# Filter rows of the "plus" side in one transfer of long rows, and the filter product as one VectorE op for each part of the filter

## The chip, the cores and the metric

The kernel runs on one core of a Trainium2 chip. The metric is device time in microseconds (us); each kernel was run several times, and all runs quoted are in the fast state (granted TensorE clock 0.986 to 1.0 in the profiled runs). Before the change the median was 134.44 us over 3 runs.

The profile shows the work of five engines, each with its own instruction stream in the program. In this kernel PE does the matmuls (786 in the profile before) and writes the memory PSUM. VectorE (DVE in the profile, 127 instructions) and ScalarE (ACT, 146) read PSUM and write the memory SBUF; such a copy out of PSUM is called an eviction. GpSimd (POOL, 33) works on tiles in SBUF here. SyncE (SP) issues nearly all transfers (DMA). The program fixes the order of each stream and lets streams wait for each other through semaphores. The kernel uses PSUM as 8 banks.

## The reference, cut to what matters

```python
# x: (1, 2048, 512) bf16;  w_r, w_i: (2048, 257) bf16
X = rfft2(layernorm(x));  X = X * (w_r + 1j * w_i)        # <- the filter
h = x + irfft2(X)
y = h + token_mlp(layernorm(h))                            # w1: 2048x1376, w2: 1376x2048
```

The kernel makes the two transforms as matmuls with constant matrices. The filter has a real part `w_r` and an imaginary part `w_i`. In the filter step the groups of 257 frequencies are handled in eight stages u = 0..7, four groups to a stage. In each stage:

1. `f2`: matmuls from Y, evicted by ScalarE as CS (two evictions per stage, `cs_2u` and `cs_2u+1`);
2. `x`: eight matmuls from CS into two PSUM banks. I write x(u) for those of stage u;
3. `v`: VectorE multiplies the PSUM result with both parts of the filter and writes V to SBUF. I write V(u);
4. `g1`: sixteen matmuls from V, evicted by ScalarE as PQ.

After stage 7 come g2, g3, a second layernorm, and the two large matmuls of the MLP.

## The kernel before

The author's builder records operations with their costs and priorities. A list scheduler then fixes each engine's order and the PSUM banks, once, from modelled durations. So a change in one operation can move others.

```python
# PSUM classes: how many units of each may be open at once
K = Builder(nc, {"f1": 6, "f2": 2, "x": 2, "g1": 2, ...})

add("W", [NP, NG, 2, LW], bf, rw)          # filter in SBUF: partition, group, part, 257
V_SPLIT = (0, 7)                            # stages whose product is made in two halves

# filter loads, in three chunks of stages; per part w and component comp (cut: minus rows, row 32)
for w, dram in ((0, A_w_r), (1, A_w_i)):
    for comp in range(2):
        d = W[comp::4, g0:g0 + ng, w, :]    # 32 partitions, rows of 257 bf16 = 514 B
        lst.append(dma(f"ld_wp{ch}_{w}{comp}", d, bass.AP(dram.tensor, g0 * LW, [[64 * LW, 32], [LW, ng], [1, LW]]), ...))
...
# the product: one VectorE op for both parts (two halves in stages 0 and 7)
wt = W[:, g0 + h * ng:g0 + h * ng + ng, :, :]
win = bass.AP(wt.tensor, wt.offset + 1, [list(wt.ap[0]), [LW, 2 * ng], [1, 2], [2, NP]])
vout = V[:, g0 + h * ng:g0 + h * ng + ng, :, :].rearrange("p g w l -> p (g w l)")
def tt(eng, bank, ...):
    s = bass.AP(s.tensor, s.offset, [list(s.ap[0]), [256, ng], [0, 2], [1, 256]])   # PSUM, each group read twice
    return eng.tensor_tensor(vout, s, win, ALU.mult)
K.op(f"v_{u}_{h}", "dve", tt, ins=[wt], outs=[vout], occ=50.0 + 2130.0 / nh, lat=170.0 + 2130.0 / nh, ...)
```

## Time and profile before

| | before |
|---|---|
| time, median of 3 (range) | 134.44 us (134.16 to 134.53) |
| profiled span, mean clock | 133.0 us, 1.000 |
| VectorE from 22 to 40 us | busy 17.88 of 18.00 us |
| V ops | 10 (six of 2048 elements, four of 1024) |
| packets of all transfers | 16,648 |

The first view is the page's packet line and its group line for V. Columns of a group line: line, engine, operation, output<-inputs, shapes, count; then busy us and mean ns of one; then idle time before them and what ended most of it.

```profile
DMA packets 16648, 22.16 MB, mean 167 GB/s; under 512 B 2720, under 2 KB 12960, under 8 KB 16128
...
L735 DVE TENSOR_TENSOR V<-ps,W 128x2048 bf16<-128x2048 f32 (+1 forms) x10 | 17.9, 1856 | 0.9 <-PE ps L527 0.9
```

The timeline of VectorE (start, us, engine, line, operation, count, and in brackets idle before it and what ended that) shows the stretch without a break:

```profile
20.39 0.69 DVE L708 CAST CS<-ps 128x512 bf16<-128x512 f32 x1 [0.92 <-PE ps L527]
22.02 17.88 DVE L735 TENSOR_TENSOR V<-ps,W 128x1024 bf16<-128x1024 f32 x10 [0.93 <-PE ps L527]
43.17 0.42 DVE L786 TENSOR_TENSOR TT<-ps,X 128x256 f32<-128x256 f32 x1 [3.27 <-PE ps L527]
```

Ten products follow one another from 22.02 to 39.90 us. Then VectorE has nothing for 3.27 us while g1, PQ, g2, EO and g3 run. V's only wait is the 0.93 us before the first, and it is for PE, not for a transfer.

The chain of waits that ended last (start, us, what):

```profile
19.15 2.77 PE ps L527 x25
...
22.02 1.04 DVE V L735
...
23.16 15.62 DVE V L735 x8
...
68.59 61.14 PE ps L527 x282
```

V lies on the chain op by op. From 43.17 to 68.5 VectorE is on it again (second layernorm), and the end is 61 us of PE without a gap.

PE's timeline around x(6), the seventh block of eight "CS,EM" matmuls:

```profile
34.66 0.61 PE L527 MATMUL ps<-CS,EM 64*128 64x256 bf16 x8
35.21 0.39 PE L527 MATMUL ps<-EM,Y 128*128 128x256 bf16 x2
35.44 0.72 PE L527 MATMUL ps<-EM,V 128*128 128x128 bf16 x10
```

x(6) is done at 35.27 us, while VectorE still works on V(5) (V(6) starts at 35.34, so x(6) is ready only just in time); the g1 matmuls that wait for V(5) stand behind it, at 35.44. So V(6) can follow V(5) at once.

SyncE's issues of the last filter loads and of the MLP's weights (both tensors appear as W):

```profile
22.61 3.28 SPq L517 DMA_DIRECT2D W<-in_A_w_i_dram  x4
...
30.52 16.34 SPq L517 DMA_DIRECT2D W<-in_B_w_dram  x15
```

### The profile page before, as it was taken

To read this page: it belongs to the slowest core of one execution; us is meant where nothing else is said; L and a number is where in the kernel's file an instruction comes from. 1 tells how busy PE (TensorE), PEld (TensorE's weight loads), DVE (VectorE), ACT (ScalarE), POOL (GpSimd) and SP (SyncE) were. 2 spreads that over 40 slices of the span, in tenths; PEclk is the share of its full clock that TensorE was granted. 3 is DMA by queue.
4 is the path that set the end of the run, shared out by engine and by line. 5 is a ranking of instruction groups with operands and counts; after the bars stand their busy time and mean duration, and the time that the engine had idled before them with its cause. 6 is when DMAs were issued, how large, how long until landed. Compare 5 with 4: busy or idle time off the path is not lost.

```text
span 133.0 us, 2023 instructions
## 1 busy us (share of the span) xinstructions
PE 125.4 (94%) x786; PEld 75.3 (57%) x786; DVE 69.2 (52%) x127; ACT 63.4 (48%) x146; POOL 12.2 (9%) x33
## 2 busy tenths in 40 slices
PE   6999989999987979999999999999999999999990
PEld 2356756878656726644434444456666666666660
DVE  0379975999990999999970000000242332423322
ACT  4569976878966999986679322222000000000000
POOL 0288830000300000000000000000000000000000
PEclk9999999999999999999999999999999999999999
DMA  3999698999999999992000000000111112111121
GB/s 94 335 370 382 178 276 229 304 317 264 411 430 430 398 411 409 419 281 89 0 0 0 0 0 0 5 0 0 39 39 64 55 39 81 42 59 59 39 79 39
DMA packets 16648, 22.16 MB, mean 167 GB/s; under 512 B 2720, under 2 KB 12960, under 8 KB 16128
## 3 DMA queue, kind: packets, MB, share of 16 engines
q1 hardware_dynamic: 16352, 21.52, 47.3%
q10 hardware_dynamic: 288, 0.52, 1.3%
q8 instruction: 6, 0.10, 0.3%
q14 instruction: 2, 0.02, 0.0%
HBM read 19.95 MB, written 2.10 MB: 166 GB/s over the span
## 4 chain that ended last, share of the span: by engine, by line
PE 51%; DVE 33%; ACT 8%; DMA 5%; issue 1%; SPq 1%; DVEq 0%; ACTq 0%
PE ps L527 50%; DVE V L735 13%; DVE H L795 7%; DMA X<-in_A_x_dram 5%; ACT Y L545 5%; DVE TT L786 4%; DVE TT L788 4%; DVE HH L800 4%; ACT rs L545 1%; ACT FS L545 1%; DVE st L649 1%; SPq L517 1%; DVE OUT L825 1%; ACT PQ L545 0%; PE ps L617 0%
## 5 line engine op out<-in xcount | busy, mean ns | idle before, releaser
L527 PE MATMUL ps<-HH,W 128*128 128x512 bf16 (+1 forms) x176 | 40.7, 379 | 1.2 <-DVE HH L800 0.9
L527 PE MATMUL ps<-GT,W 128*128 128x512 bf16 (+1 forms) x176 | 38.2, 379 | 0.0
L825 DVE SCALAR_TENSOR_TENSOR OUT<-ps,B2f,H 128x512 bf16<-128x512 f32 x16 | 12.0, 750 | 48.7 <-PE ps L527 48.7
L527 PEld LDWEIGHTS ps<-GT,W 128*128 128x128 bf16 (+1 forms) x176 | 25.4, 144 | 12.7
L527 PEld LDWEIGHTS ps<-HH,W 128*128 128x128 bf16 (+1 forms) x176 | 17.2, 100 | 21.2 <-DVE HH L800 1.9
L735 DVE TENSOR_TENSOR V<-ps,W 128x2048 bf16<-128x2048 f32 (+1 forms) x10 | 17.9, 1856 | 0.9 <-PE ps L527 0.9
L545 ACT ACTIVATE GT<-ps,B1f 128x512 bf16<-128x512 f32 (+1 forms) x11 | 7.1, 688 | 14.6 <-PE ps L527 14.6
L545 ACT ACTIVATE JK<-H,nm 128x512 bf16<-128x512 bf16 x16 | 11.6, 724 | 3.0 <-DVE H L795 2.9
L617 PE MATMUL ps<-ZT 128*128 128x512 bf16 x34 | 11.3, 479 | 1.3 <-DVE ZT L613 1.2
L649 DVE BATCH_NORM_STATS2 st<-X 128x6 f32<-128x512 bf16 x14 | 9.3, 668 | 5.3 <-DMA X<-in_A_x_dram 5.3
L795 DVE TENSOR_TENSOR H<-ps,TT 128x512 bf16<-128x512 f32 x16 | 10.9, 681 | 0.0
L545 ACT ACTIVATE PQ<-ps 128x512 bf16<-128x512 f32 x16 | 8.9, 603 | 3.5 <-PE ps L527 3.2
L545 ACT ACTIVATE EO<-ps 128x512 bf16<-128x512 f32 x16 | 9.3, 599 | 0.9 <-PE ps L527 0.9
L527 PE MATMUL ps<-EM,V 128*128 128x128 bf16 x128 | 9.2, 219 | 0.5 <-DVE V L735 0.5
L527 PE MATMUL ps<-EM,PQ 128*128 128x256 bf16 x64 | 9.0, 273 | 0.7 <-ACT PQ L545 0.7
L545 ACT ACTIVATE CS<-ps 128x512 bf16<-128x512 f32 x15 | 8.3, 608 | 2.1 <-PE ps L527 2.1
L527 PE MATMUL ps<-EM,Y 128*128 128x256 bf16 x64 | 8.7, 273 | 0.4 <-ACT Y L545 0.4
L527 PEld LDWEIGHTS ps<-EM,V 128*128 128x128 bf16 x128 | 7.5, 98 | 2.3 <-issue 1.4
L629 POOL TENSOR_SCALAR FS<-FP,rs 128x256 bf16<-128x256 bf16 x9 | 8.3, 935 | 1.3 <-ACT rs L545 1.3
L527 PE MATMUL ps<-FS,X 128*128 128x256 bf16 x64 | 8.3, 273 | 0.1
L786 DVE TENSOR_TENSOR TT<-ps,X 128x256 f32<-128x256 f32 x16 | 6.7, 416 | 3.3 <-PE ps L527 3.3
L527 PEld LDWEIGHTS ps<-EM,PQ 128*128 128x128 bf16 x64 | 6.2, 98 | 2.9 <-ACT PQ L545 0.9
(36 smaller groups left out, 80.3 us busy)
## 6 DMA issues: line engine op xcount, KB each, us to landing
W<-in_B_w_dram SPq DMA_DIRECT2D x4, 1376.0 KB, 11.0
W<-in_B_w_dram SPq DMA_DIRECT2D x10, 512.0 KB, 17.6
out_dram<-OUT SPq DMA_DIRECT2D x16, 128.0 KB, 1.7
W<-in_A_w_r_dram SPq DMA_DIRECT2D x4, 257.0 KB, 4.3
W<-in_A_w_i_dram SPq DMA_DIRECT2D x4, 257.0 KB, 5.0
X<-in_A_x_dram SPq DMA_DIRECT2D x4, 256.0 KB, 5.8
X<-in_A_x_dram SPq DMA_DIRECT2D x2, 512.0 KB, 7.7
W<-in_A_w_r_dram SPq DMA_DIRECT2D x4, 192.8 KB, 3.5
```

The lines of the kernel that those rows point to most:

```text
L517: return eng.dma_start(dst, src)
L527: return K.op(name, "pe", lambda eng, bank: eng.matmul(outf(bank), lhsT, rhs, start=start, stop=stop), ins=ins or [lhsT, rhs], occ=occ, la ...
L545: return eng.activation(dst, s, func, **kw)
L617: return K.op(name, "pe", lambda eng, bank: eng.matmul(ps[:, bank, :], ZT[:, 0:NP], ZT[:, :], start=True, stop=True), ins=[ZT[:, :]], occ= ...
L629: dve(f"fs{i}", lambda eng, bank: eng.tensor_scalar(FS[:, i, :, :], FP[:, i, :, :], rs, None, op0=ALU.mult), [FP[:, i, :, :], rs], [FS[:, ...
L649: dve(f"st_{i}", lambda eng, bank, i=i, x=x: eng.bn_stats(ST[:, i, 0:6], x), [x], [ST[:, i, 0:6]], 512, prio=25)
L735: return eng.tensor_tensor(vout, s, win, ALU.mult)
L786: dve(f"tl_{s2}", lambda eng, bank, tt=tt, xl=xl: eng.tensor_tensor(tt[:, 0, :], ps[:, bank, 256:512], xl, ALU.add), [xl], [tt[:, 0, :]], ...
L788: dve(f"th_{s2}", lambda eng, bank, tt=tt, xh=xh: eng.tensor_tensor(tt[:, 1, :], xh, ps[:, bank, 256:512], ALU.subtract), [xh], [tt[:, 1, ...
L795: return eng.tensor_tensor(hs.rearrange("p (h d) -> p h d", h=2), e, tt[:, :, :], ALU.add)
L800: dve(f"hh_{s2}", lambda eng, bank, s2=s2, hs=hs: eng.tensor_scalar(HH[:, s2, :], hs, NM[:, s2:s2 + 1], R2[:, s2:s2 + 1], op0=ALU.add, op1 ...
L825: dve(f"fin{s2}", lambda eng, bank, dst=dst, bia=bia, hs=hs: eng.scalar_tensor_tensor(dst, ps[:, bank, :], bia, hs, op0=ALU.add, op1=ALU.add),
```

## The change

The intent: rows of the filter that lie side by side in DRAM should lie side by side in SBUF too, so that a transfer moves rows of 4, 12 or 16 times 514 B, and both components (which need the same rows) come in one transfer. For that the part index w moves outward in SBUF, and the order of the 128 output rows is permuted. With w outermost, the product's filter operand for both parts would have one dimension more; that this cannot be a single op was the author's view. So the product becomes one op per part: 20 ops instead of 10, with the same elements in all.

```diff
-    return 4 * (k2 * 2 + s) + 2 * sign + comp
+    return 4 * (k2 * 2 + s) + 2 * comp + sign
...
-    add("W", [NP, NG, 2, LW], bf, rw)
+    add("W", [NP, 2, NG, LW], bf, rw)
...
+            d = W[0:NP:2, w, g0:g0 + ng, :].rearrange("p g l -> p (g l)")
+            lst.append(dma(f"ld_wp{ch}_{w}", d, bass.AP(dram.tensor, g0 * LW, [[64 * LW, 32], [0, 2], [1, ng * LW]]),
+                           64 * ng * 514, prio=42 - ch, group=f"w{ch}"))
             for comp in range(2):
-                d = W[comp::4, g0:g0 + ng, w, :]
-                lst.append(dma(f"ld_wp{ch}_{w}{comp}", d, bass.AP(dram.tensor, g0 * LW, [[64 * LW, 32], [LW, ng], [1, LW]]), ...
                 # minus rows: as before, 514 B each, to W[1 + 2 * comp::4, w, h0:h0 + nh, :]
...
-            K.op(f"v_{u}_{h}", "dve", tt, ins=[wt], outs=[vout], occ=50.0 + 2130.0 / nh, ...)
+            for w in range(2):
+                win = bass.AP(wt.tensor, wt.offset + 1, [list(wt.ap[0]), [LW, ng], [1, 2], [2, NP]])
+                vout = V[:, g0 + h * ng:g0 + h * ng + ng, w, :].rearrange("p g (y j) -> p g y j", y=2)
+                ...
+                K.op(f"v_{u}_{h}{w}", "dve", tt, ins=[wt], outs=[vout], occ=50.0 + 1065.0 / nh, ...)
```

More of the change, by code (lines that the diff above doesn't have):

```diff
@@ L578, in build_kernel @@
         for w, dram in ((0, A_w_r), (1, A_w_i)):
+            d = W[0:NP:2, w, g0:g0 + ng, :].rearrange("p g l -> p (g l)")
+            lst.append(dma(f"ld_wp{ch}_{w}", d, bass.AP(dram.tensor, g0 * LW, [[64 * LW, 32], [0, 2], [1, ng * LW]]),
+                           64 * ng * 514, prio=42 - ch, group=f"w{ch}"))
+            h0, nh = (g0, ng) if g0 else (1, ng - 1)
             for comp in range(2):
-                d = W[comp::4, g0:g0 + ng, w, :]
-                lst.append(dma(f"ld_wp{ch}_{w}{comp}", d, bass.AP(dram.tensor, g0 * LW, [[64 * LW, 32], [LW, ng], [1, LW]]),
-                               32 * ng * 514, prio=42 - ch, group=f"w{ch}", rate=300.0))
-                h0, nh = (g0, ng) if g0 else (1, ng - 1)
-                d = W[2 + comp::4, h0:h0 + nh, w, :]
+                d = W[1 + 2 * comp::4, w, h0:h0 + nh, :]
                 lst.append(dma(f"ld_wm{ch}_{w}{comp}", d, bass.AP(dram.tensor, (64 - h0) * LW, [[64 * LW, 32], [-LW, nh], [1, LW]]),
                                32 * nh * 514, prio=42 - ch, group=f"w{ch}", rate=300.0))
-                if g0 == 0:
-                    d = W[2 + comp::4, 0, w, :]
-                    lst.append(dma(f"ld_wz{ch}_{w}{comp}", d, bass.AP(dram.tensor, 32 * LW, [[64 * LW, 32], [1, LW]]),
-                                   32 * 514, prio=42 - ch, group=f"w{ch}", rate=300.0))
+            if g0 == 0:
+                d = W[1:NP:2, w, 0, :]
+                lst.append(dma(f"ld_wz{ch}_{w}", d, bass.AP(dram.tensor, 32 * LW, [[64 * LW, 32], [0, 2], [1, LW]]),
+                               64 * 514, prio=42 - ch, group=f"w{ch}", rate=300.0))
         for u in range(u0, u1):
@@ L727, in stage_x, with tt @@
         for h in range(nh):
-            wt = W[:, g0 + h * ng:g0 + h * ng + ng, :, :]
-            win = bass.AP(wt.tensor, wt.offset + 1, [list(wt.ap[0]), [LW, 2 * ng], [1, 2], [2, NP]])
-            vout = V[:, g0 + h * ng:g0 + h * ng + ng, :, :].rearrange("p g w l -> p (g w l)")
-            def tt(eng, bank, h=h, win=win, vout=vout):
-                s = psf[:, bank * 512 + h * 512:bank * 512 + h * 512 + 256 * ng]
-                s = bass.AP(s.tensor, s.offset, [list(s.ap[0]), [256, ng], [0, 2], [1, 256]])
-                return eng.tensor_tensor(vout, s, win, ALU.mult)
-            K.op(f"v_{u}_{h}", "dve", tt, ins=[wt], outs=[vout], occ=50.0 + 2130.0 / nh, lat=170.0 + 2130.0 / nh, unit=unit, pr=True,
-                 last=h == nh - 1, prio=11, after=wload[u])
+            for w in range(2):
+                wt = W[:, w, g0 + h * ng:g0 + h * ng + ng, :]
+                win = bass.AP(wt.tensor, wt.offset + 1, [list(wt.ap[0]), [LW, ng], [1, 2], [2, NP]])
+                vout = V[:, g0 + h * ng:g0 + h * ng + ng, w, :].rearrange("p g (y j) -> p g y j", y=2)
+                def tt(eng, bank, h=h, win=win, vout=vout):
+                    s = psf[:, bank * 512 + h * 512:bank * 512 + h * 512 + 256 * ng].rearrange("p (g y j) -> p g y j", g=ng, y=2)
+                    return eng.tensor_tensor(vout, s, win, ALU.mult)
+                K.op(f"v_{u}_{h}{w}", "dve", tt, ins=[wt], outs=[vout], occ=50.0 + 1065.0 / nh, lat=170.0 + 1065.0 / nh, unit=unit, pr=True,
+                     last=h == nh - 1 and w == 1, prio=11, after=wload[u])
     lastg1 = [None]
```

## The prediction

> **What bounds the kernel now.** The chain of waits has four stretches: to 22.0 us statistics, scaling and ScalarE's evictions Y; from 22.02 to 39.9 us VectorE's ten products V<-ps,W back to back; from 43.2 to 68.5 us VectorE again (TT, H, HH); then 61 us of PE without a gap. In the windows table VectorE is busy 17.88 of the 18.0 us from 22 to 40, and the wait table has a single wait of V, 0.93 us for PE before the first one. No V waits for a filter transfer: W's transfers take from issue to landing 5 us in the median, SyncE issues the last at about 25 us, and the products never pause. So filter transfers are off the chain, while V is on it, op by op.
>
> **Removed.** W needs 8,192 rows of 514 B. The plus half becomes 384 long rows, so the page's 16,648 packets should fall by about 3,700, and 28 issues of W (5.7 to 25.9 us on SyncE, about 0.7 us each) become 20. The filters land some us earlier and w1 starts near 25 us instead of 30.5. [...]here the stretch 20 to 30 us, mostly such rows, moved 284 GB/s against 387 later, so longer rows should gain. But nothing on the chain waits for it: worth 0.
>
> **Added.** Ten more VectorE ops, six of 2048 elements becoming twelve of 1024 and four of 1024 eight of 512. The trace has 2.28 us for 2048 and 1.21 for 1024[...]. Ops that follow one another overlap: H with 512 elements starts the next after 0.60, about 0.07 over its elements. Ten ops: +0.7 us, all on the chain.
>
> **Moved.** The order of PE's instructions changes, and here I expect the larger cost. Before, the matmuls x for stage u=6 (input of the eighth product) stand before the g1 matmuls that wait for V of u=5. After, they stand behind the g1 matmul that waits for the *second* product of u=5. So after V(5) VectorE must idle: wake-up 0.14, three g1 matmuls 0.2, eight x matmuls 0.61, start of V 0.14, about 1.0 us (estimate from the timeline of before). Elsewhere x(u+2) waits for the last product of u while V(u+1) runs for 2.3 us: hidden.
>
> **Sum.** +0.7 +1.0 = +1.7 us on the chain in 22 to 40 us; what follows (3.3 us of g1, PQ, g2, EO, g3; VectorE's 25 us; PE's 61 us) is shifted unchanged. Predicted 136.1 us, range 135.2 to 137.0; faster by 2% 0.02, within 0.90, slower 0.08.
>
> **What would show it.** V group: 20 ops, about 19.4 us busy summed, 1.21 and 0.68 us each. A wait V<-PE of about 1 us before the fifteenth V op (u=6), none for DMA. Last V ends about 41.6 instead of 39.9. PE's last stretch still about 61 us. W1's first issue about 5 us earlier with no effect.
>
> **What would make it wrong.** More V waits on PE, if ScalarE's reordered CS/PQ evictions are late (136.5 to 137.5); x(6) ready although PE's order says not (135.1);[...] or the early part waiting on filters in a way the trace hides, which would make the transfers worth something.

Ten ops at 0.07 us are +0.7, the hole is +1.0, and 134.44 + 1.7 gives 136.1 us. The 0.07 follows from the trace of before alone: V ops of 2048 elements last 2.28 us and those of 1024 last 1.21, so 512 elements more take about 0.53 us (an estimate, (2.28 - 1.21) / 2), and H, with 512 elements, starts the next op after 0.60 us. That longer rows should gain was the inference from the 284 and 387 GB/s (20 to 30 and 30 to 45 us).

## The result

| | before | after |
|---|---|---|
| time, median of 4 (range) | 134.49 us (134.16 to 134.55) | 136.10 us (136.06 to 136.16) |
| profiled span, mean clock | 133.0 us, 1.000 | 134.2 us, 0.998 |
| V, from first start to last end | 22.02 to 39.90: 17.88 us | 21.90 to 41.46: 19.56 us |
| first TT after V | 43.17 us | 44.61 us |

The run before appears here with a fourth time, so its median differs from that above. The ratio after to before is 1.0125, 95% interval 1.0108 to 1.0143, which is "same" at the 2% limit but clearly not equal. Ratios here and below are the mean time of one kernel's fast runs over that of the other's of the same rounds, so they are not quite the ratio of the medians that I quote. Intervals are 95%.

The page's lines, after. There are 3,840 packets fewer, and twice the V ops:

```profile
DMA packets 12808, 22.16 MB, mean 165 GB/s; under 512 B 2592, under 2 KB 8736, under 8 KB 12160
...
L735 DVE TENSOR_TENSOR V<-ps,W 128x1024 bf16<-128x1024 f32 (+1 forms) x20 | 18.5, 1001 | 1.9 <-PE ps L527 1.9
```

VectorE's timeline, after:

```profile
20.27 0.69 DVE L708 CAST CS<-ps 128x512 bf16<-128x512 f32 x1 [0.92 <-PE ps L527]
21.90 13.80 DVE L735 TENSOR_TENSOR V<-ps,W 128x512 bf16<-128x512 f32 x14 [0.93 <-PE ps L527]
36.71 4.75 DVE L735 TENSOR_TENSOR V<-ps,W 128x1024 bf16<-128x1024 f32 x6 [1.01 <-PE ps L527]
44.61 0.42 DVE L786 TENSOR_TENSOR TT<-ps,X 128x256 f32<-128x256 f32 x1 [3.16 <-PE ps L527]
```

The stretch is 1.68 us longer. It splits in two: 13.80 + 4.75 = 18.55 us of products, 0.67 more than before, and one hole of 1.01 us before the fifteenth V op, which is V(6). The hole is a wait for PE.

PE's timeline around the hole, after. The "CS,EM" block at 36.03 is x(6), the one at 37.24 is x(7):

```profile
34.87 1.03 PE L527 MATMUL ps<-EM,Y 128*128 128x256 bf16 x8
35.75 0.34 PE L527 MATMUL ps<-EM,V 128*128 128x128 bf16 x3
36.03 0.61 PE L527 MATMUL ps<-CS,EM 64*128 64x256 bf16 x8
36.57 0.73 PE L527 MATMUL ps<-EM,V 128*128 128x128 bf16 x10
37.24 0.61 PE L527 MATMUL ps<-CS,EM 64*128 64x256 bf16 x8
```

V(5) ends at 35.70. Three g1 matmuls that waited for it start at 35.75, x(6) follows at 36.03 and is done at 36.64, and V(6) starts at 36.71. ScalarE's timeline of the same time:

```profile
34.24 1.08 ACT L545 ACTIVATE PQ<-ps 128x512 bf16<-128x512 f32 x2 [0.22 <-PE ps L527]
35.21 1.58 ACT L545 ACTIVATE CS<-ps 128x512 bf16<-128x512 f32 x3
```

The first of these three CS evictions (start 35.21) is cs_13, the later of the two that x(6) reads. With 0.60 us for one it ends at about 35.8. So it too was only just ready. This is a hint that PE's order alone may not be the whole cause; the experiments take it up.

The chain of waits, after, shows PE where it showed V before:

```profile
19.04 6.68 PE ps L527 x72
...
29.98 1.21 DVE V L735
...
33.52 3.16 PE ps L527 x39
...
36.71 3.56 DVE V L735 x4
...
70.03 8.81 PE ps L527 x40
```

A learner should not read this as "PE is now the limit from 19 to 36 us". The chain is followed back from the wait at 36.71 through PE's stream, in which instructions stand one behind the other; VectorE was busy all the time up to 35.70.

SyncE's issues, after:

```profile
17.10 2.19 SPq L517 DMA_DIRECT2D W<-in_A_w_i_dram  x3
...
26.74 16.36 SPq L517 DMA_DIRECT2D W<-in_B_w_dram  x15
```

The last filter loads are issued 6.6 us earlier (by 19.3 instead of 25.9 us) and the first MLP weights 3.8 us earlier. From 5 to 26 us the core moved 362 GB/s, against 293 before; these runs do not separate the longer rows from the fewer issues. V waits for no transfer in either trace.

### The profile page after: what moved, and what is told of

It reads as the page before. It is cut to its first block, busy times and chain, and to the rows that moved or that the text cites. A ratio compares the mean times of both kernels' runs of the same rounds, so it can differ in the third digit from the quotient of the medians.

```text
span 134.2 us, 2017 instructions
## 1 busy us (share of the span) xinstructions
PE 124.3 (93%) x776; PEld 74.4 (55%) x786; DVE 69.8 (52%) x137; ACT 63.9 (48%) x146; POOL 12.1 (9%) x33
## 4 chain that ended last, share of the span: by engine, by line
PE 59%; DVE 24%; ACT 8%; DMA 5%; issue 1%; SPq 1%; ACTq 0%
PE ps L527 59%; DVE H L795 7%; ACT Y L545 5%; DMA X<-in_A_x_dram 5%; DVE TT L786 4%; DVE TT L788 4%; DVE HH L800 4%; DVE V L735 4%; ACT rs L545 1%; ACT PQ L545 1%; ACT FS L545 1%; DVE st L649 1%; SPq L517 1%; DVE OUT L825 1%; PE ps L617 0%
## 5 line engine op out<-in xcount | busy, mean ns | idle before, releaser
L735 DVE TENSOR_TENSOR V<-ps,W 128x1024 bf16<-128x1024 f32 (+1 forms) x20 | 18.5, 1001 | 1.9 <-PE ps L527 1.9
L527 PE MATMUL ps<-EM,V 128*128 128x128 bf16 x128 | 10.8, 220 | 1.2 <-DVE V L735 1.2
L617 PE MATMUL ps<-ZT 128*128 128x512 bf16 x32 | 9.4, 430 | 1.6 <-DVE ZT L613 1.2
L527 PE MATMUL ps<-EM,Y 128*128 128x256 bf16 x64 | 9.4, 274 | 0.7 <-ACT Y L545 0.4
L527 PEld LDWEIGHTS ps<-FS,X 128*128 128x128 bf16 x64 | 5.6, 97 | 4.1 <-POOL FS L629 2.6
```

The costliest lines, as they stand in the source:

```text
L527: return K.op(name, "pe", lambda eng, bank: eng.matmul(outf(bank), lhsT, rhs, start=start, stop=stop), ins=ins or [lhsT, rhs], occ=occ, la ...
L617: return K.op(name, "pe", lambda eng, bank: eng.matmul(ps[:, bank, :], ZT[:, 0:NP], ZT[:, :], start=True, stop=True), ins=[ZT[:, :]], occ= ...
```

## The experiments

The theory to be tested: (a) ten further VectorE instructions cost about 0.67 us; (b) the order that the scheduler chose costs about 1.0 us; (c) the transfers are worth nothing. The rivals: the loss comes from the new layout or from collisions with faster transfers; or the hole has another cause than PE's order, since, as I found when I listed the dependencies of each kernel, the eviction CS and the PSUM banks tie x(6) to V(5) too. The tie by CS runs through PE: the last f2 matmul for cs_13 stands behind a g1 matmul that waits for the first product of stage 5. As for the banks, in the changed kernel x(6) was given the two banks that V(5) reads; in every earlier stage x(u+2) takes the banks of V(u).

All twelve kernels gave correct results. Below, "V stretch" is from the first V's start to the last V's end, and "hole" is VectorE's idle time inside it; all are of the profiled run.

### 1. The changed kernel, in the order of the kernel before (order_kept)

Each product stays one op for the scheduler, and its emit function issues both instructions.

```diff
-            for w in range(2):
-                ... K.op(f"v_{u}_{h}{w}", ..., occ=50.0 + 1065.0 / nh, ...)
+            def tt(eng, bank, ...):
+                for w in range(2):
+                    ... ins = eng.tensor_tensor(vt[:, :, w, :]..., s, win, ALU.mult)
+                return ins
+            K.op(f"v_{u}_{h}", ..., occ=50.0 + 2130.0 / nh, ...)
```

> The changed kernel, but each product is scheduled as one op that issues two VectorE instructions, so PE, ScalarE and the PSUM banks keep the order and the choice of the kernel before. Theory (ten more instructions cost about 0.67 us, the order costs about 1.0, transfers nothing): 20 V instructions of 1.21 and 0.68 us, no idle before any V but the first, V stretch about 18.55 us, time about 135.1 us. Rival 1 (the instructions or the new layout cost all of it, by a slower access pattern or a collision with the faster transfers): 136.1. Rival 2 (the order is all of it): 134.5.

Measured: 135.11 us against 134.42, ratio 1.0049 (1.0036 to 1.0062). VectorE's timeline has one row for all twenty:

```profile
22.00 18.45 DVE L735 TENSOR_TENSOR V<-ps,W 128x512 bf16<-128x512 f32 x20 [0.93 <-PE ps L527]
```

No hole is left, and V takes 18.45 us. So the instructions cost 0.57 us in this trace (18.45 - 17.88) and 0.69 us in the medians, and the rest of the loss, 1.0 us, is the order. Both rivals fall.

### 2. The split alone, with the old layout and the old transfers (split_only)

```diff
-            wt = W[:, g0 + h * ng:g0 + h * ng + ng, :, :]
-            win = bass.AP(wt.tensor, wt.offset + 1, [list(wt.ap[0]), [LW, 2 * ng], [1, 2], [2, NP]])
+            for w in range(2):
+                wt = W[:, g0 + h * ng:g0 + h * ng + ng, w, :]
+                win = bass.AP(wt.tensor, wt.offset + 1, [list(wt.ap[0]), [2 * LW, ng], [1, 2], [2, NP]])
```

> The kernel before, with its layout of the filter and its 28 short-row transfers, and only the product split in two; the scheduler then gives PE and ScalarE the changed kernel's order, instruction by instruction. Theory (the transfers are worth nothing, all of the loss is the split and its order): 136.1 us, V stretch 19.56 us with one idle of about 1.0, first W1 issue about 30.5 us. Rival (long rows hide some loss, or the new layout costs something): 136.6 or more, or 135.6 or less.

Measured: 135.96 us against 134.43, ratio 1.0115 (1.0100 to 1.0129); the changed kernel's interval was 1.0108 to 1.0143. The hole is the same:

```profile
21.95 13.80 DVE L735 TENSOR_TENSOR V<-ps,W 128x512 bf16<-128x512 f32 x14 [0.93 <-PE ps L527]
36.75 4.75 DVE L735 TENSOR_TENSOR V<-ps,W 128x1024 bf16<-128x1024 f32 x6 [1.01 <-PE ps L527]
```

PE's and ScalarE's instructions stand in exactly the order of the changed kernel, the packets are again 16,648, and the first MLP weights are issued at 30.11 us. The two rows of V are as long as in the changed kernel (13.80 and 4.75 us), so the layout changes nothing in the products either. So the split makes the whole loss, and the shorter or longer rows change the time by nothing that these runs can tell.

### 3. PE's order at x(6), undone in the changed kernel (x_first)

```diff
+    move("pe", [f"x_{G}_{c}{r}" for G in (12, 13) for c in range(2) for r in range(2)], before="g1_20_01")
```

> The changed kernel with only the eight matmuls x of stage 6 moved ahead of the three g1 matmuls that wait for the second product of stage 5; PSUM banks and ScalarE's order stay. As the prediction put it (x stands behind that g1 in PE's order, and this is the cause): the idle second goes, 135.1 us. Rival (x(6) also was given the PSUM banks that the products of stage 5 read, and its CS eviction comes only about then; PE's order is but one of three ties): idle falls only by the three g1 matmuls, from 1.01 to about 0.8 us, time about 135.9.

Measured: 136.09 us against 134.42, ratio 1.0121 (1.0105 to 1.0137).

```profile
36.69 4.75 DVE L735 TENSOR_TENSOR V<-ps,W 128x1024 bf16<-128x1024 f32 x6 [0.84 <-PE ps L527]
```

The hole shrinks only from 1.01 to 0.84 us, as the rival said, and the time does not move. Undoing PE's order alone, as the prediction named it, does not close the hole. Of the two ties left, the eviction ends last here: V(5) ends at 35.85 (22.05 + 13.80), cs_13 at about 35.95, and x(6) starts at 36.02.

### 4. ScalarE's order and PE's f2 mended as well, banks left (x_cs_first)

```diff
+    move("pe", [f2 of CS 12 and 13], before="g1_16_01")
+    move("act", ["cs_12", "cs_13"], before="pq_4_0")
+    move("pe", [x(6)], before="g1_20_00")
```

> The changed kernel with PE's f2 of stage 6 moved ahead of the g1 of stage 4, ScalarE's CS evictions 12 and 13 ahead of PQ, and x(6) ahead of all g1 of stage 5: both orders are then right for x(6), but its two PSUM banks are still those that the products of stage 5 read. If the orders alone are the cause: no idle before the fifteenth V, 135.1 us. If the banks hold it as well: idle of about 0.75 us (wake-up 0.14, eight x matmuls 0.6), time about 135.8 to 135.9.

Measured: 136.05 us against 134.42, ratio 1.0122 (1.0108 to 1.0135). PE's and VectorE's timelines of this run, in this order:

```profile
35.71 0.61 PE L527 MATMUL ps<-CS,EM 64*128 64x256 bf16 x8 [0.93 <-ACT PQ L545]
```

```profile
36.38 4.94 DVE L735 TENSOR_TENSOR V<-ps,W 128x1024 bf16<-128x1024 f32 x6 [0.81 <-PE ps L527]
```

V(5) ends at 35.57 here (21.77 + 13.80), and x(6) starts 0.14 us later, at 35.71. PE had idled for 0.93 us in front of it, and the eviction that x(6) reads had ended at 34.64 (start 34.04, 0.60 long). The view names ScalarE as the releaser, but by then the only wait left in the program was that for V(5) by way of the banks: the listed dependencies of x(6) are the two CS evictions, one load of constants and V(5). This run also shows a small cost of the edit itself: the last six V ops take 4.94 instead of 4.75 us, because f2 of stage 7 now stands behind x(6) (x(7) starts at 38.16 us, in run 3 at 37.39).

### 5. Orders and banks mended (x_banks)

As run 4, with f2 of stage 7 also ahead of the g1 of stage 5, and the banks exchanged:

```diff
+    rebank("x_12_00", 6, was=V(5), now=V(4))     # x(6) on the banks that V(4) read, as other stages do
+    rebank("g1_20_00", 2, ...); rebank("g1_22_00", 3, ...)   # g1 of stage 5 on the banks that V(5) read
+    ...                                           # cut: four later units that change banks with them
```

> The changed kernel with PE's and ScalarE's order mended for stage 6 as in the run before (f2 of stages 6 and 7 also ahead of the g1 of stage 5) and with x(6) on the two PSUM banks that the products of stage 4 read, g1 of stage 5 on those of stage 5. If three ties (PE's order, ScalarE's order, the banks) hold x(6) and nothing else does: no idle before any V but the first, V stretch about 18.55 us, time about 135.1 us. Rival (something else, such as the evictions' rate, holds it): idle stays above 0.5 us, time 135.7 or more.

Measured: 135.08 us against 134.43, ratio 1.0051 (1.0037 to 1.0064).

```profile
21.97 18.47 DVE L735 TENSOR_TENSOR V<-ps,W 128x512 bf16<-128x512 f32 x20 [0.93 <-PE ps L527]
```

The hole is gone, and the V stretch is that of run 1. Runs 3, 4 and 5 together: mending PE's order leaves 0.84 us of the hole, mending ScalarE's order too leaves 0.81, and only with the banks it closes. Run 5 also moved f2 of stage 7; in run 4 that stands behind x(6) in PE's stream, so it cannot be what held x(6). Whether the banks alone, with both orders left as they were, would have closed it was not run; with PE's order left, the g1 that waits for V(5) stands in front, and the next run shows that this is enough to make a hole.

### 6. The prediction's step alone, put into the kernel before (x_late_before)

```diff
+    move("pe", [x(6)], before="g1_21_01")
```

> The kernel before (whole products, its banks, its ScalarE order) with only the eight x matmuls of stage 6 moved behind the first three g1 matmuls of stage 5. This is the step that the prediction named, alone. Theory: VectorE idles about 1.0 us before the eighth V op, no more instructions, time about 135.4 to 135.5 us. Rival (PE's order alone does little, as mending it alone did little): 134.4 to 134.7.

Measured: 135.66 us against 134.43, ratio 1.0091 (1.0076 to 1.0107); V stretch 19.09 us. PE's and VectorE's timelines:

```profile
35.37 0.44 PE L527 MATMUL ps<-EM,V 128*128 128x128 bf16 x5 [0.68 <-DVE V L735]
35.74 0.61 PE L527 MATMUL ps<-CS,EM 64*128 64x256 bf16 x8
```

```profile
36.42 4.55 DVE L735 TENSOR_TENSOR V<-ps,W 128x2048 bf16<-128x2048 f32 x3 [1.20 <-PE ps L527]
```

Whole products, old banks, old ScalarE order: eight matmuls a few places later in PE's stream cost 1.2 us. That is a little more than the 1.0 expected, at least in part because my edit put x(6) behind five g1 matmuls (0.37 us from 35.37 to 35.74) and not behind three as I had written. So PE's order is enough by itself to make the hole, and by run 4 so are the banks; whether ScalarE's order alone would be enough was not run. This is why undoing one tie (run 3) showed almost nothing: a null result from undoing one of several causes does not clear that cause.

### 7. Four instructions per product (four_ops)

Run 1 with each product in four instructions, by part and by half of the groups.

```diff
-                for w in range(2):
+                for w, q in ((0, 0), (0, 1), (1, 0), (1, 1)):
```

> The changed kernel in the order of the kernel before (as in the run that kept the order), each product as four VectorE instructions by part of the filter and by half of its groups: 40 instructions in place of 10. Theory (each further instruction costs about 0.067 us on VectorE, nothing else): V stretch about 17.88 + 30 x 0.067 = 19.9 us, no idle, time about 136.4 us. Rival (the cost of 0.6 us in the kept order is the first split or the layout, not a price per instruction): time near 135.1.

Measured: 136.49 us against 134.43, ratio 1.0151 (1.0136 to 1.0166). V stretch 19.74 us (21.96 to 41.70) without a hole: (19.74 - 17.88) / 30 = 0.062 us for each further instruction; run 1 gives (18.45 - 17.88) / 10 = 0.057. So there is a price per instruction, nearly the same from 10 to 20 and from 10 to 40.

### 8. A mend through the scheduler that failed (f2_first)

I first looked for a one-number mend: a higher priority for f2, after which no x(u) depended on V(u-1).

```diff
-                       unit, b == 0, b == 1, par == 0 and b == 0, 10, 256)
+                       unit, b == 0, b == 1, par == 0 and b == 0, 14, 256)
```

> The changed kernel with one number changed: the scheduler's priority of the matmuls f2 is raised from 10 to 14, after which every x(u) depends, by order and by PSUM bank, on the products of stage u-2 at latest, x(6) too. Theory (the idle second is made by the order that the scheduler chose, not by the split itself): no idle before the fifteenth V, V stretch about 18.55 us, time about 135.1. Rival (evictions by ScalarE cannot keep up with the split product whatever the order): idle stays about 1 us somewhere in the V stretch, time about 136.1.

Measured: 140.55 us against 134.42, ratio 1.0477 (1.0443 to 1.0512), a clear miss.

```profile
26.70 2.49 DVE L735 TENSOR_TENSOR V<-ps,W 128x512 bf16<-128x512 f32 x4 [5.56 <-PE ps L527]
29.84 16.06 DVE L735 TENSOR_TENSOR V<-ps,W 128x1024 bf16<-128x1024 f32 x16 [0.65 <-PE ps L527]
```

The later holes are indeed gone (sixteen products in one row), but the first product starts at 26.70 instead of 21.90 us, since PE now makes 48 of the 64 f2 matmuls before x(0) is complete at 26.60, with one or two x matmuls at a time between them. I had checked only which V each x depends on, and not when the first x comes. The run says nothing against the theory, and nothing for it.

### 9. Tries at a version that beats both (pool_24, pool_2, pool_13, pool_2b)

If the stretch is VectorE's time for elements, work could leave VectorE. From the kernel before: in stages 2 and 4 (or 2; or 1 and 3) ScalarE copies the result of x to SBUF as bf16, VectorE makes the product with the first part only, and GpSimd the second from SBUF.

```diff
+        if u in OFF:
+            cp = act(f"xs_{u}", xs, <PSUM of x(u)>, ACT.Copy, 1024, ...)
+            K.op(f"v_{u}_0", "dve", <product with part 0>, ..., after=wload[u] + [cp])
+            K.op(f"vp_{u}", "pool", <product of xs with part 1>, ...)
+            return
```

> Not a test of the change but a try at a version that beats both, since the runs say that the stretch is VectorE's time for elements: the kernel before, where in stages 2 and 4 the product with the second part of the filter leaves VectorE. ScalarE copies the 128x1024 result of x from PSUM to SBUF as bf16 (about 1.0 us each, an estimate from its 0.6 us for 512), then VectorE makes the first part's product alone (1.14 us in place of 2.23) and GpSimd the second from SBUF[...]. VectorE's work falls by 2.2 us; one wait of about 1 us is expected before V of stage 5, whose x depends on the op just before it. If that holds: 133.0 to 133.8 us. Rival: ScalarE, busy 14.1 of the 18 us, or the x, V, copy order takes it all back: 134.4 to 136.

> As the run beside it, with stage 2 alone. VectorE's work falls by 1.1 us; the order again puts one x (stage 4) behind the op just before its own product, about 1 us of wait. Expected 133.8 to 134.5 us if only that wait is paid; above 134.6 if ScalarE's extra copy delays more than one stage.

Measured: pool_24 135.00 us against 134.52, ratio 1.0043 (1.0026 to 1.0059); pool_2 134.84, ratio 1.0022 (1.0010 to 1.0034). In pool_24 V ends at 39.96 us, as before the change: the 2.2 us that VectorE saved came back as holes of 0.33 and 1.76 us; in pool_2 the holes are 0.33 and 1.00 us. Both times missed the hoped-for ranges; pool_24 lies in the range of its rival, pool_2 above the 134.6 that its text gave as the mark of delay by ScalarE's copy. GpSimd's product took 2.07 us, less than half of the 4.5 us that I had told the scheduler, a guess that no run had shown. With that number, a cheaper eviction in the model, and stages chosen so that no x depends on the op just before its own product:

> The try at a faster version again: stages 1 and 3 leave their second product to GpSimd, the scheduler is told what the last two runs measured (2.07 us for GpSimd's product) and an eviction cost nearer the trace for CS and PQ, and the plan was chosen because no x depends, by order or bank, on the op just before its own product. If the waits of the two runs before came from such ties: VectorE's V stretch about 17.9 - 2.2 = 15.7 us with little idle, time 132.2 to 133.2 us. Rival (ScalarE, with two more copies of 1.03 us, sets the pace of that stretch): idle of 1 us or more before V ops, 133.4 to 134.6.

> As the run beside it with stage 2 alone: V stretch about 16.8 us with little idle, time 133.3 to 133.9 us. Rival: idle again, 134.2 or more.

Measured: pool_13 134.69 us against 134.47, ratio 1.0016 (1.0004 to 1.0029); pool_2b 135.13, ratio 1.0046 (1.0032 to 1.0059). Both missed again. pool_2b is as its rival said; pool_13 is slightly above its rival's range (133.4 to 134.6), and none of its holes reaches the 1 us that the rival named. In the table by stretch (us, then busy of PE, PEld, DVE, ACT, POOL with counts, clock, DMA share, GB/s), first the kernel before, then pool_13:

```profile
22.00:40.00 18.00, 17.25 (x225) 13.08 (x224) 17.88 (x10) 14.14 (x27) 1.22 (x7) 1.00 1.07 340
```

```profile
22.00:40.00 18.00, 17.14 (x225) 13.09 (x223) 16.04 (x10) 15.81 (x29) 6.68 (x16) 1.00 1.02 326
```

VectorE's 17.88 us fell to 16.04, but ScalarE rose from 14.14 to 15.81, PE stayed at 17.1, and V in pool_13 ends at 40.01 us, so the stretch did not shorten; its holes are 0.76, 0.36, 0.62 and 0.17 us long. Which of ScalarE and PE's order holds it now was not separated. No version that beats the kernel before was found.

## Why the prediction was right, point by point

| step of the prediction | predicted | measured |
|---|---|---|
| total | 136.1 us (135.2 to 137.0) | 136.10 |
| ten instructions | +0.7 us | +0.57 in V's stretch, +0.69 in the medians (run 1) |
| hole before the fifteenth V op | about 1.0 us | 1.01; removing it is worth 0.9 to 1.0 us (136.10 or 135.96 against 135.1) |
| transfers | 0 | 135.96 without, 136.10 with them, 95% intervals overlap |
| last V ends | about 41.6 us | 41.46 |
| packets | about 3,700 fewer | 3,840 fewer (the 128 beyond the 3,712 of the rows are all under 512 B; not looked into) |
| first MLP weights issued | near 25 us | 26.74 (before: 30.52) |
| last stretch of PE | about 61 us | 70.03 to 131.20: 61.2 us |

- **What bounds the kernel** was read right: VectorE's row without a break, and V's single wait, for PE. That the faster filter loads are worth nothing is shown by run 2.
- **The added ops**: the prediction took 0.07 us per op from the H ops and named all of it on the chain. Runs 1 and 7 measure 0.057 and 0.062. The ops of the new pattern last as long as those of the old one with as many elements: 1215 ns for 1024 (before 1217). One number of the "what would show it" part was wrong: I gave 19.4 us as the summed busy time, but 12 x 1.21 + 8 x 0.68 is 20.0 (the page's mean of 1001 ns times 20), and the page's 18.5 counts overlaps once. It entered no other figure.
- **The moved order**: the place and the size of the hole were right, and the parts nearly: wake-up of PE 0.05 us (35.70 to 35.75; predicted 0.14), three g1 0.28 (0.2), x(6) 0.61 (0.61), start of V 0.07 (0.14), together 1.01. What was incomplete is the cause. The prediction says of x(6) that it stands "behind the g1 matmul that waits for the *second* product of u=5". That alone is enough (run 6), but it was not alone: mending just that left 0.84 us (run 3). x(6) was also tied by the CS eviction order and by its PSUM banks (runs 4 and 5). That it did not harm the number is luck: the three ties end close together (banks free at 35.70, eviction done at about 35.8, g1 past at 36.03); as advice for a mend it would have failed. Why the scheduler planned stage 6 so late stays open: with evictions 10 to 50 ns cheaper in its model the plan still had x(6) behind V(5) (listed, not run).
- **Elsewhere hidden**: right; the wait table has two waits of V for PE in all, 1.9 us, that before the first V and this one.

## What to carry to other kernels

Ask first what the busy engine waits for. Here it ran without a break, so ten more instructions on it cost 0.6 us, and nothing waited for the transfers, so 3,840 packets fewer were worth 0. If a scheduler orders the program, compare the order of the *other* engines too: for every op on the bounding engine, ask which of its own earlier ops its inputs depend on, through the stream order of the producers, through their inputs, and through the PSUM banks. If that is the op just before it, expect a hole, as here before V(6) (1.01 us); where several ties end together, as here, undoing one does not close it (0.84 us were left in run 3).
